# One bundle of moves at the first routing: an earlier trace of one load, a later register load, a count in two products

## The chip, the cores and the metric

One core of one Trainium2 chip. The metric is device time in microseconds (us) of one launch, lower is better. Before the change three runs took 764.91, 766.84 and 766.99 us.

## What is computed

Three layers in a row, all in float32: attention with random features, a mixture of experts with one expert per token, and a wide gated layer.

```
q_p, k_p = phi(q * scale), phi(k * scale)      # 128 exponential features per row of 64, row maximum taken off
kv = einsum('bhsm,bhsd->bhmd', k_p, v); z = sum(k_p, axis=2)
x = (q_p . kv) / (q_p . z + 1e-06)             # 4 batches x 8 heads x 576 rows x 64  ->  2304 x 512
expert = argmax(x @ w_gate); probs = softmax(x @ w_gate)
y[e] = probs[e] * (relu(x @ w1[e]) @ w2[e])    # 8 experts, 512 -> 1024 -> 512
out = (g @ w_out), g = h * sigmoid(1.702 h), h = y @ w_in      # 512 -> 2048 -> 512
```

## The kernel before, in words

The work of attention is cut into eight groups: group i holds four heads of batch i // 2. For each group `load_qk` (L247) brings k or q as a tile `m`, `halves_T` (L296) makes from it the tile `xT` with the 64 columns on the partitions, and `ph_P` multiplies it with omega. The first five tiles are turned by TensorE; the other eleven are split into two float16 halves (ScalarE the high one, L307, GpSimd the low one, L308: tile `hl`) and turned by a DMA that SyncE issues (`DMA_TRANSPOSE`, L309). `xT` has three buffers, so the turned k of group 4 takes the buffer of q of group 2 and can't start before TensorE's last read of that.

`kgen` (L390) makes the features of k in five steps (0, 1, 4, 2, 3) and `kv_ps`; `qgen` (L414) makes the features of q (steps P, tile `pr`, `qp`), turns them (X, tile `tq`), multiplies by kv (N, tile `num`) and turns the result (R, tiles `tx` and `small`), in the order of `Q_ORDER`. `route` (L523) finds a batch's most used expert: it counts the tokens of each expert with a product of ones with the one-hot matrix `oh` (`ct_ps`, L561), takes the largest (`es`), and loads it into a register of SyncE (`values_load`, L604), which the weight loads (`stage`, L674, tile `st`) use as an address. ScalarE and VectorE or GpSimd split each weight tile in two halves (`wh` L698, `wl` L700), and `moe_gen` multiplies (`m_ps`, L136).

`attention_gen` merges qgen(i), kgen(i + 1) and, after each second group, the route of the batch just finished; from the first route on, the routed expert's products are woven in by a ratio of costs. The text gives the order of tracing only: a scheduler that plays the program on its own clock sets each engine's order from it, so an edit at one place can reorder all engines behind it. In qgen(2) the k of group 4 is asked for at n == KPRE, the seventh step:

```
            if n == KPRE and i + 2 < NQ:
                load_qk(k, k_in, i + 2, asked[-1] if i == QB + 1 else None)
                halves_T(k_in, i + 2, nc.vector if i + 2 < DVE_LO else nc.gpsimd)
```

The PSUM tag "n" has one buffer, which `lg_ps`, `ct_ps` and, from group 2 on, every `num` share; "u" has one, for `tq` and `tx`; the `pr` tiles share three ("a").

Names below: P3 is the last projection of q of group 2; N0 to N4 are the `num` products of that group.

Of the kernel before, what the change touches and what calls it, by code (L numbers as in the profile page):

```python
# [22 lines left out]
def kernel(  # L23
# [13 lines left out]
    nc = tc.nc  # L37
# [6 lines left out]
    T = 4  # L44
    TAIL = S - T * P
# [16 lines left out]
    XQ = nc.sync  # L62
    DVE_LO = 1
    KPRE = 6
# [78 lines left out]
    ones = const.tile([P, P], F32, name="ones")  # L143
# [38 lines left out]
    NJ = 9  # L182
    QB = H // QH
    NQ = B * QB
    asked = []
    clock = [0]
    late = []

# [77 lines left out]
    def square_sum(m, c, sq, folds):  # L266
        nc.gpsimd.tensor_tensor(out=m[:, c], in0=m[:, c], in1=m[:, c], op=ALU.mult)
        w = D
        for _ in range(folds):
            w //= 2  # L270
            o = sq[:, c].unsqueeze(2) if w == 1 else m[:, c, 0:w]
            nc.gpsimd.tensor_tensor(out=o, in0=m[:, c, 0:w], in1=m[:, c, w:2 * w], op=ALU.add)
        if w > 1:
            nc.vector.tensor_reduce(out=sq[:, c], in_=m[:, c, 0:w], axis=AX.X, op=ALU.add)
        nc.scalar.activation(out=sq[:, c], in_=sq[:, c], func=ACTF.Copy, scale=sq_scale)
# [20 lines left out]
    def halves_T(src, i, eng):  # L296
        sides[0] += 1
        if sides[0] <= FPX:
            return turned(src, i)
        if sides[0] - 1 in LO_DVE:  # L300
            eng = nc.vector
        m = src[i]
        hl = att.tile([P, NB, 2, D], F16, tag="hl", name="hl", bufs=2)
        xT = att.tile([P, NB, P], F16, tag="xT", name="xT", bufs=3)
        sq = att.tile([P, NB], F32, tag="sq", name="sq", bufs=3)
        for c in (slice(0, 8), slice(8, NB)) if i < FINE else (slice(0, NB),):
            nc.scalar.activation(out=hl[:, c, 0], in_=m[:, c], func=ACTF.Copy)  # L307
            eng.tensor_tensor(out=hl[:, c, 1], in0=m[:, c], in1=hl[:, c, 0], op=ALU.subtract)  # L308
            XQ.dma_start_transpose(out=xT[:, c], in_=hl[:, c].rearrange("p n a d -> p (n a d)"))  # L309
            square_sum(m, c, sq, FOLD_LATE)  # L310
        src[i] = (xT, sq, False)

# [15 lines left out]
    turn = {"N": 0, "X": 0, "A": 0}  # L328
# [85 lines left out]
    def qgen(i):  # L414
        b, qd = divmod(i, H // QH)
        qi = i
        if i + 1 < NQ:
            load_qk(q, q_in, i + 1)
            halves_T(q_in, i + 1, nc.vector if i + 1 < DVE_LO else nc.gpsimd)
# [60 lines left out]
        for n, op in enumerate(Q_ORDER.split()):  # L480
            g = int(op[1])
            if op == "R0" and qd == 0:
                while x_done[0] < b - 1:
                    yield None
                xh_t[b] = (moe if b % 2 else xep).tile([P, KD, S], F32R, tag="xh", name="xh", bufs=1)
                xl_t[b] = (moe if b % 2 else xep).tile([P, KD, S], F32R, tag="xl", name="xl", bufs=1)
            if op[0] == "P":
                c = ph_P(i, src, qp, "qp", 3, g)
            else:
                c = {"X": X, "N": N, "R": XT}[op[0]](g)  # L490
            if n == 0 and i + 1 < NQ:
                load_v(i + 1)
            if n == KPRE and i + 2 < NQ:
                load_qk(k, k_in, i + 2, asked[-1] if i == QB + 1 else None)
                halves_T(k_in, i + 2, nc.vector if i + 2 < DVE_LO else nc.gpsimd)
            yield c
# [23 lines left out]
    def route_steps(b):  # L520
# [3 lines left out]
        for hf, tg in ((0, "n"), (1, "u")):  # L524
            c = slice(hf * HS, (hf + 1) * HS)
# [9 lines left out]
        for t in range(T + 1):  # L535
            n = P if t < T else TAIL
# [12 lines left out]
        nc.vector.tensor_reduce(out=rm, in_=lg, axis=AX.X, op=ALU.max)  # L549
        oh = att.tile([P, T + 1, E], F32, tag="oh", name="oh", bufs=2)  # L550
        nc.vector.tensor_tensor(out=oh, in0=lg, in1=rm.to_broadcast([P, T + 1, E]), op=ALU.is_equal)
        nc.vector.memset(oh[TAIL:, T, :], 0.0)
        ex = att.tile([P, T + 1, E], F32, tag="ex", name="ex", bufs=2)
        nc.vector.tensor_tensor(
            out=ex, in0=lg, in1=rm.to_broadcast([P, T + 1, E]), op=ALU.subtract
# [2 lines left out]
        yield 0.5  # L558
        yield 0
        ct_ps = pp.tile([P, T + 1, E], F32, tag="n", name="ct_ps", bufs=1)  # L560
        nc.tensor.matmul(  # L561
            out=ct_ps.rearrange("p t e -> p (t e)"), lhsT=ones, rhs=oh.rearrange("p t e -> p (t e)")
        )
        ct = att.tile([P, E], F32, tag="ct", name="ct", bufs=2)
        nc.vector.tensor_reduce(out=ct, in_=ct_ps.rearrange("p t e -> p e t"), axis=AX.X, op=ALU.add)
        cm = att.tile([P, 8], F32, tag="cm", name="cm", bufs=2)
# [9 lines left out]
        if b == B - 1:  # L576
            dg = att.tile([P, T * P + TAIL], F32, tag="dg", name="dg", bufs=1)
            for t in range(T + 1):
                n = P if t < T else TAIL
                nc.scalar.activation(  # L580
                    out=dg[:n, t * P:t * P + n], in_=ident[:n, :n], func=ACTF.Copy, scale=gate[:n, t, :]
# [5 lines left out]
        for t in range(T + 1):  # L587
# [9 lines left out]
            out=rr[:, :, 0:1], in0=eq, scalar=-float(2 * E), in1=ixf, op0=ALU.mult, op1=ALU.add  # L597
# [3 lines left out]
        nc.vector.tensor_tensor(out=total, in0=total, in1=hit, op=ALU.subtract)  # L601
        nc.vector.tensor_copy(rr[:, :, 1:2], gate)
        yield 0.5
        reg_t[b] = nc.values_load(  # L604
            es[0:1, 0:1], engines=[mybir.EngineType.SP], min_val=0, max_val=E - 1,
            skip_runtime_bounds_check_because="an index of the largest of E counts",
        )
        pump()
        nc.sync.dma_start(
            out=r_dram[b * S:b * S + T * P].rearrange("(p t) c -> p t c", t=T), in_=rr[:, 0:T]  # L610
# [70 lines left out]
    def pump(n=0):  # L681
        ahead = 2 * NW - 1 if prep["split"] < 2 else NST
        while prep["staged"] < min(max(prep["split"] + ahead, 2 * NW - 1), 2 * NW * B) and prep["staged"] // (2 * NW) in reg_t:
            stage(*divmod(prep["staged"], 2 * NW))
            prep["staged"] += 1
        while n and prep["split"] < min(prep["free"], prep["staged"]):
            split_w(*divmod(prep["split"], 2 * NW))
            prep["split"] += 1
            n -= 1
# [310 lines left out]
    if True:  # L1000
# [26 lines left out]
        while a_live:  # L1027
            if force == "a" or (force is None and done_a - lead <= A_RATIO * done_m):
                c = next(A, "end")
# [5 lines left out]
            else:  # L1035
                c = next(Mg)
# [363 lines left out]
        p = hp.tile([P, SETW], F32R, tag="y2", name="p2", bufs=1)  # L1400
# [29 lines left out]
    with tc.If(more > 0), tc.tile_pool(name="gp", bufs=1) as gp:  # L1430
        with tc.For_i(0, NT // P, 1) as w:
# [7 lines left out]
            xT = gp.tile([P, KD, P], F32, name="xT")  # L1439
# [13 lines left out]
            with tc.For_i(0, E, 1) as e:  # L1453
# [6 lines left out]
                with tc.If(cnt > 0):  # L1460
# [3 lines left out]
                    for f in range(NF1):  # L1464
                        wa = gp.tile([P, KD, P], F32, name="wa", bufs=2)
                        nc.sync.dma_start(
                            out=wa,
                            in_=w1[bass.ds(e, 1), :, f * P:(f + 1) * P].rearrange(
                                "o (k p) f -> p (o k) f", p=P
                            ),  # L1470
                        )
                        ps = pp.tile([P, P], F32, tag="m", name="g_ps", bufs=2)
                        for kk in range(KD):
                            nc.tensor.matmul(
                                out=ps, lhsT=wa[:, kk], rhs=xT[:, kk], start=(kk == 0), stop=(kk == KD - 1)
# [4 lines left out]
                    for dt in range(KD):  # L1480
                        wb = gp.tile([P, NF1, P], F32, name="wb", bufs=2)
                        nc.sync.dma_start(
                            out=wb,
                            in_=w2[bass.ds(e, 1), :, dt * P:(dt + 1) * P].rearrange(
                                "o (k p) d -> p (o k) d", p=P
                            ),
                        )
                        ps = pp.tile([P, P], F32, tag="m", name="g_ps", bufs=2)
                        for f in range(NF1):
                            nc.tensor.matmul(  # L1490
                                out=ps, lhsT=wb[:, f], rhs=ha[:, f], start=(f == 0), stop=(f == NF1 - 1)
# [6 lines left out]
                    for f in range(NF2):  # L1498
                        wh, wl = general_w(gp, f, 0)
                        oh, ol = general_w(gp, f, 1)  # L1500
# [44 lines left out]
```

## Time and profile before

| what | value |
|---|---|
| runs | 764.91, 766.84, 766.99 us, median 766.84 |
| the profiled execution | 766.79 us, its span 764.9 us |
| TensorE (PE) busy | 737.1 us, 96% |
| VectorE (DVE), ScalarE (ACT), GpSimd (POOL) busy | 527.5, 337.5, 131.8 us |
| weight tiles of the routed expert | 31 loads of 512 KB and 2 of 256 KB |

The page gives the busy time of each engine, the waits tell which instruction stood idle for whom, the timeline shows single instructions with start and length, and the windows add busy time and the granted TensorE clock for a stretch. Times are counted from the start of the span. A matmul's length in the timeline covers its whole way through a pipeline; the distance between starts is what one costs in a row. A `num` or `ct_ps` product shows as two records there (x4 in an order below is x8 in the trace).

### The profile page before, as it was taken

To read this page: it belongs to the slowest core of one execution; us is meant where nothing else is said; L and a number is where in the kernel's file an instruction comes from. 1 tells how busy PE (TensorE), PEld (TensorE's weight loads), DVE (VectorE), ACT (ScalarE), POOL (GpSimd) and SP (SyncE) were. 2 spreads that over 40 slices of the span, in tenths; PEclk is the share of its full clock that TensorE was granted. 3 is DMA by queue.
4 is the path that set the end of the run, shared out by engine and by line. 5 is a ranking of instruction groups with operands and counts; after the bars stand their busy time and mean duration, and the time that the engine had idled before them with its cause. 6 is when DMAs were issued, how large, how long until landed. Compare 5 with 4: busy or idle time off the path is not lost.

```text
span 764.9 us, 14360 instructions
## 1 busy us (share of the span) xinstructions
PE 737.1 (96%) x5559; PEld 715.1 (93%) x5559; DVE 527.5 (69%) x1188; ACT 337.5 (44%) x638; POOL 131.8 (17%) x78
## 2 busy tenths in 40 slices
PE   7998799998999999999999999999999999999997
PEld 6877789998999999998999999999999999999996
DVE  5866848583958577655879559981368777777774
ACT  5554554334623423332427565454576443444331
POOL 3563467604900522000000000000000000000000
PEclk9999799999999999999999999999999999999999
DMA  5447495539723544558155548972978544443311
GB/s 156 116 134 187 160 234 110 136 83 250 189 71 98 169 164 141 175 172 274 59 165 197 178 167 299 320 259 101 330 276 297 171 138 138 138 126 121 114 30 31
DMA packets 136715, 127.57 MB, mean 167 GB/s; under 512 B 58176, under 2 KB 120896, under 8 KB 135744
## 3 DMA queue, kind: packets, MB, share of 16 engines
q1 hardware_dynamic: 123936, 98.85, 44.6%
q10 hardware_dynamic: 12704, 27.73, 10.5%
q8 instruction: 45, 0.74, 0.4%
q14 instruction: 30, 0.25, 0.1%
HBM read 79.68 MB, written 40.40 MB: 157 GB/s over the span
## 4 chain that ended last, share of the span: by engine, by line
PE 80%; DMA 7%; DVE 5%; POOL 3%; ACT 2%; issue 2%; SPq 1%; ACTq 0%; POOLq 0%; DVEq 0%
PE m_ps L136 17%; PE qa L1249 13%; PE qa L1146 13%; PE qm L1249 7%; PE w_ps L136 5%; DMA st<-in_moe_w_dram 4%; PE pb L1249 3%; PE qm L1146 3%; PE qu L1146 3%; PE num L444 2%; POOL wl L700 2%; PE kv_ps L402 2%; PE qn L1146 2%; PE qt L1146 2%; DMA m<-in_k_dram 1%
## 5 line engine op out<-in xcount | busy, mean ns | idle before, releaser
L1146 PE MATMUL qa<-y,wi 128*128 128x384 f32 x576 | 109.2, 337 | 0.4 <-DVE g L901 0.4
L1146 PEld LDWEIGHTS qa<-y,wi 128*128 128x128 f32 x576 | 101.4, 188 | 0.8 <-DVE g L901 0.8
L136 PE MATMUL m_ps<-xh,wh 128*128 128x288 f32 x256 | 77.8, 304 | 0.7 <-DVE h1l L735 0.7
L136 PE MATMUL m_ps<-xh,wl 128*128 128x288 f32 x256 | 76.0, 298 | 0.0
L136 PE MATMUL m_ps<-xl,wh 128*128 128x288 f32 x256 | 75.8, 296 | 0.0
L700 POOL TENSOR_TENSOR wl<-st,wh 128x1024 fp32r<-128x1024 f32 x23 | 55.1, 2403 | 108.2 <-ACT wh L698 108.2
L359 DVE TENSOR_REDUCE small<-pr 128x4 f32<-128x512 f32 (+1 forms) x80 | 51.0, 638 | 16.1 <-PE pr L351 12.3
L698 ACT ACTIVATE wh<-st 128x1024 fp32r<-128x1024 f32 (+1 forms) x33 | 34.0, 1033 | 44.0 <-DMA st<-in_moe_w_dram 32.7
L735 DVE SCALAR_TENSOR_TENSOR h1l<-m_ps,h1h 128x288 fp32r<-128x288 f32 x64 | 28.9, 454 | 34.0 <-ACT h1h L732 34.0
L732 ACT ACTIVATE h1h<-m_ps 128x288 fp32r<-128x288 f32 x64 | 25.8, 405 | 55.3 <-PE m_ps L136 53.9
L136 PEld LDWEIGHTS m_ps<-xh,wh 128*128 128x128 f32 x256 | 48.1, 188 | 1.7 <-DVE h1l L735 1.4
L136 PE MATMUL m_ps<-h1h,wh 128*128 128x288 f32 x160 | 49.2, 307 | 0.0
L136 PEld LDWEIGHTS m_ps<-xl,wh 128*128 128x128 f32 x256 | 48.1, 188 | 0.1
L136 PEld LDWEIGHTS m_ps<-xh,wl 128*128 128x128 f32 x256 | 48.0, 188 | 0.2
L136 PE MATMUL m_ps<-h1h,wl 128*128 128x288 f32 x160 | 47.7, 298 | 0.3 <-POOL wl L700 0.3
L136 PE MATMUL m_ps<-h1l,wh 128*128 128x288 f32 x160 | 47.6, 297 | 0.0
L1249 PE MATMUL qa<-p,p 128*128 128x256 f32 x360 | 46.1, 282 | 1.1 <-DVE p L855 0.8
L1249 PE MATMUL qa<-p,gs 128*128 128x256 f32 x360 | 45.9, 282 | 0.0
L1249 PEld LDWEIGHTS qa<-p,p 128*128 128x128 f32 x360 | 44.1, 189 | 1.6 <-DVE p L855 1.0
L1249 PEld LDWEIGHTS qa<-p,gs 128*128 128x128 f32 x360 | 44.2, 189 | 0.0
L432 ACT ACTIVATE qpT<-tq 128x512 f32<-128x512 f32 (+1 forms) x40 | 22.1, 552 | 43.3 <-PE tq L430 38.6
L444 PE MATMUL num<-kv,qpT 128*128 128x65 f32 (+1 forms) x320 | 39.4, 267 | 0.7 <-ACT qpT L432 0.6
(213 smaller groups left out, 1835.1 us busy)
## 6 DMA issues: line engine op xcount, KB each, us to landing
g_dram<-g ACTq DMA_DIRECT2D x48, 384.0 KB, 3.9
st<-in_moe_w_dram SPq DMA_DIRECT2D x31, 512.0 KB, 5.0
pg<-g_dram SPq DMA_DIRECT2D x10, 1024.0 KB, 5.5
raw<-in_moe_w_in_dram SPq DMA_DIRECT2D x16, 512.0 KB, 3.8
gt<-g_dram SPq DMA_DIRECT2D x8, 1024.0 KB, 5.4
p<-wo_dram SPq DMA_DIRECT2D x6, 1024.0 KB, 7.3
yt<-y_dram SPq DMA_DIRECT2D x12, 384.0 KB, 5.4
vm<-in_v_dram SPq DMA_DIRECT2D x32, 128.0 KB, 3.2
```

The source lines that it names most:

```text
L136: ins = nc.tensor.matmul(out=ps, lhsT=a, rhs=b, start=start and n == 0, stop=stop and n == 2)
L359: nc.vector.tensor_reduce(out=pm, in_=ps[:, :w], axis=AX.X, op=ALU.max, negate=on_act)
L402: nc.tensor.matmul(out=kv_ps[:, h, :], lhsT=kp[j // 2][:, j % 2, h2, :], rhs=vm[:, h, t, :], start=(t == 0), stop=False,)
L432: nc.scalar.activation(out=qt[i][:, :w], in_=tq[:, :w], func=ACTF.Exp)
L444: nc.tensor.matmul(out=ps[:n, c, h2, :], lhsT=lhsT, rhs=kv[:, h, :])
L698: nc.scalar.activation(out=hi[:, :, s], in_=st[:, :, s], func=ACTF.Copy)
L700: eng.tensor_tensor(out=lo[:, :, s], in0=st[:, :, s], in1=f32(hi)[:, :, s], op=ALU.subtract)
L732: nc.scalar.activation(out=hh[:, f], in_=ps, func=ACTF.Relu)
L735: nc.vector.scalar_tensor_tensor(out=hl[:, f], in0=ps, scalar=0.0, in1=f32(hh[:, f]), op0=ALU.max, op1=ALU.subtract)
L1146: ins = nc.tensor.matmul(out=ps, lhsT=w[:, a, ks], rhs=y[:, b, kk], start=start and kk + m == 0, stop=kk == 1 and m == 2, skip_group_check ...
L1249: ins = nc.tensor.matmul(out=ps, lhsT=x[:, f], rhs=w[i][:, f], start=start and f + m == 0, stop=f == NP - 1 and m == 2, skip_group_check=True,
```

## The change

The k of group 4 is loaded and turned in the trace right after the first step of qgen(2) instead of the seventh (all other groups keep KPRE). The first batch's register load may not stand ahead of that turn on SyncE. For the first batch the clearing of the unused half of `oh` is gone; the count is two products, one over the four full tiles and one over the 64 rows of the last.

```
-    asked = []
+    asked, turned_last = [], [None]
...
-            XQ.dma_start_transpose(out=xT[:, c], in_=hl[:, c].rearrange("p n a d -> p (n a d)"))
+            turned_last[0] = XQ.dma_start_transpose(out=xT[:, c], in_=hl[:, c].rearrange("p n a d -> p (n a d)"))
...
-            if n == KPRE and i + 2 < NQ:
+            if n == (0 if i == QB else KPRE) and i + 2 < NQ:
...
-        nc.vector.memset(oh[TAIL:, T, :], 0.0)
+        if b:
+            nc.vector.memset(oh[TAIL:, T, :], 0.0)
...
+        full = T if b == 0 else T + 1
         nc.tensor.matmul(
-            out=ct_ps.rearrange("p t e -> p (t e)"), lhsT=ones, rhs=oh.rearrange("p t e -> p (t e)")
+            out=ct_ps[:, 0:full].rearrange("p t e -> p (t e)"), lhsT=ones,
+            rhs=oh[:, 0:full].rearrange("p t e -> p (t e)"),
         )
+        if b == 0:
+            nc.tensor.matmul(out=ct_ps[:, T], lhsT=ones[:TAIL, :], rhs=oh[:TAIL, T])
...
+        seen = len(nc.cur_bb.bb.instructions)
         reg_t[b] = nc.values_load(
             es[0:1, 0:1], engines=[mybir.EngineType.SP], min_val=0, max_val=E - 1,
...
+        if b == 0:
+            for x in nc.cur_bb.bb.instructions[seen:]:
+                tc.add_manual_dep(
+                    x, turned_last[0].ins.name,
+                    mybir.DependencyInfo(mybir.DependencyClass.NoSync, mybir.DependencyReason.DATA),
+                    reason="behind the turn",
+                )
```

SyncE, at the first routing. Before, the register load stood first, then eight weight loads, and the turn of k of group 4 (`xT_1159`) behind them; these are the last of those rows:

```order
L674 DMA st_1033<-in_moe_w2_dram 128x2x512
L609 DMA r_dram_65<-rr_1011 128x8
L674 ISA
L674 DMA st_1254<-in_moe_w2_dram 128x2x512
L612 DMA r_dram_65<-rr_1011 64x2
L309 DMA_TRANSPOSE xT_1159<-hl_1158 128x18x128
L504 DMA x_dram_63<-xn_875 64x256
L309 DMA_TRANSPOSE xT_1458<-hl_1457 128x18x128
```

Now the same turn is called `xT_902`:

```order
L258 DMA m_1453<-in_q_dram 64x2x64
L622 DMA r_dram_65<-rr_1025 128x8
L625 DMA r_dram_65<-rr_1025 64x2
L309 DMA_TRANSPOSE xT_902<-hl_901 128x18x128
L610 TENSOR_LOAD es_1000
L687 ISA
L687 DMA st_1034<-in_moe_w1_dram 128x4x128
```

The two stores of the routing result and the turn went ahead of the register load and of all weights.

TensorE, at the count (the difference, numbers of tiles left out):

```order
 L537 MATMUL lg_ps<-ident,lT 64x16
 L430 MATMUL tq<-ident,qp 128x128 x4
-L561 MATMUL ct_ps<-oh,ones 128x40
+L563 MATMUL ct_ps<-oh,ones 128x32
+L568 MATMUL ct_ps<-oh,ones 128x8
+L444 MATMUL num<-kv,qpT 128x65 x4
 L350 LDWEIGHTS xT
 L350 MATMUL pr<-wh_117,xT 128x128
```

The count became two products, and N0 came forward to stand right behind them; before, it stood behind 16 projections. Further on, the first product of the routed expert stood behind X2 and eight more projections, at row 248; now it stands at row 287, behind N4, N2 and N3, that is behind nearly all of group 2. The orders agree again over the last 1,467 of some 3,120 rows.

ScalarE, in the second batch's routing. Before (`wh2_2241` waits for a weight tile, `qpT_2331` is the last exponential of its group):

```order
L698 ACTIVATE wh1_2164<-st_2093 128x1024
L432 ACTIVATE qpT_2265<-tq_2260 128x512
L386 ACTIVATE kp_2295<-kp_2295 128x512
L386 ACTIVATE kp_2371<-kp_2371 128x512
L275 ACTIVATE sq_2496<-sq_2496 128x18
L698 ACTIVATE wh2_2241<-st_2162 128x1024
L432 ACTIVATE qpT_2331<-tq_2326 128x512
```

and now:

```order
L634 DMA row_2098<-gate_dram_64 128x640
L432 ACTIVATE qpT_2265<-tq_2260 128x512
L386 ACTIVATE kp_2295<-kp_2295 128x512
L386 ACTIVATE kp_2371<-kp_2371 128x512
L432 ACTIVATE qpT_2331<-tq_2326 128x512
L275 ACTIVATE sq_2496<-sq_2496 128x18
L711 ACTIVATE wh2_2241<-st_2162 128x1024
```

The exponential went ahead of the copy that waits for a weight tile.

## Rows read from the trace of the kernel before

**Rows 1.** Waits of TensorE, 60 to 340 us: total, times, longest.

```profile
PE ct_ps L561 <- DVE oh L552: 4.1, 1, 4.1
PE tx L464 <- ACT qpT L432: 2.2, 1, 2.2
PE pr L350 <- DMA xT<-hl: 1.9, 1, 1.9
```

**Rows 2.** Windows: length, then busy time of PE, PEld, DVE, ACT, POOL, then PEclk.

```profile
75.00:80.00 5.00, 1.20 (x12) 0.82 (x11) 4.35 (x20) 2.92 (x7) 4.84 (x4) 0.79 0.00 2
...
77.50:78.00 0.50, 0.00 (x0) 0.00 (x0) 0.50 (x3) 0.50 (x4) 0.50 (x1) 0.90 0.00 0
...
88.00:88.50 0.50, 0.50 (x9) 0.48 (x8) 0.07 (x1) 0.40 (x1) 0.00 (x0) 0.86 0.76 134
```

**Rows 3.** Timeline of VectorE (start, length, instruction), 77 to 86 us.

```profile
77.92 1.43 DVE L551 TENSOR_TENSOR oh<-lg,rm 128x40 f32<-128x40 f32 x1
...
80.10 0.07 DVE L552 MEMSET oh<- 64x8 f32 x1
...
82.36 0.18 DVE L565 TENSOR_REDUCE ct<-ct_ps 128x8 f32<-128x40 f32 x1
...
83.50 0.68 DVE L359 TENSOR_REDUCE small<-pr 128x4 f32<-128x512 f32 x1
84.10 0.14 DVE L571 CAST es<-ci 128x1 int32<-128x1 uint32 x1
...
85.47 0.17 DVE L596 SCALAR_TENSOR_TENSOR rr<-eq,ixf 128x5 f32<-128x5 f32 x1
```

**Rows 4.** Timeline of TensorE, 80 to 107 us.

```profile
80.31 0.62 PE L561 MATMUL ct_ps<-oh,ones 128*128 128x40 f32 x2 [4.12 <-DVE oh L552]
...
83.98 1.91 PE L444 MATMUL num<-kv,qpT 128*128 128x65 f32 x8
...
87.29 0.31 PE L351 MATMUL pr<-wl,xT 128*128 128x128 f16 x1
...
88.62 0.38 PE L136 MATMUL m_ps<-xh,wh 128*128 128x288 f32 x1
...
95.05 0.40 PE L136 MATMUL m_ps<-xh,wh 128*128 128x288 f32 x1
...
98.18 0.29 PE L136 MATMUL m_ps<-xh,wl 128*128 128x288 f32 x1
...
106.64 0.23 PE L350 MATMUL pr<-wh,xT 128*128 128x128 f16 x1 [1.86 <-DMA xT<-hl]
```

**Rows 5.** Timeline of SyncE's queue and of GpSimd, 70 to 100 us.

```profile
84.97 5.03 SPq L674 DMA_DIRECT2D st<-in_moe_w_dram  x8
90.10 0.88 SPq L609 DMA_DIRECT2D r_dram<-rr  x1
...
92.92 6.89 SPq L309 DMA_TRANSPOSE xT<-hl  x1
...
70.94 2.37 POOL L308 TENSOR_TENSOR hl<-m,hl 128x1152 f16<-128x1152 f32 x1 [12.70 <-DMA vm<-in_v_dram]
```

**Rows 6.** Line L309, 30 to 60 us: ns min/median/max of issuing, us to landing.

```profile
L309 SPq DMA_TRANSPOSE xT<-hl x2: 1841/2000/2160, 35.5 to 57.6; - x2
...
DMA to landing us min/median/max: 4.0/4.0/4.0
```

**Rows 7.** The same line, 90 to 107 us.

```profile
L309 SPq DMA_TRANSPOSE xT<-hl x2: 6073/6480/6886, 92.9 to 100.5; - x2
...
DMA to landing us min/median/max: 9.0/11.3/13.7
```

**Rows 8.** Timeline of ScalarE, 84 to 86 and 174 to 181 us.

```profile
84.68 1.14 ACT L376 ACTIVATE kp<-pr,mx 128x128 f32<-128x128 f32 x4 [0.65 <-DVE mx L368]
...
174.68 0.22 ACT L275 ACTIVATE sq<-sq 128x18 f32<-128x18 f32 x1
179.69 1.06 ACT L698 ACTIVATE wh<-st 128x1024 fp32r<-128x1024 f32 x1 [4.79 <-DMA st<-in_moe_w_dram]
180.65 0.58 ACT L432 ACTIVATE qpT<-tq 128x512 f32<-128x512 f32 x1
```

## The prediction

> **What bounds the kernel now.** The page comes first: TensorE is busy 737.1 of 764.9 us, so the time is its work, plus its pauses, plus what it does at half clock. The waits of TensorE say which pauses lie in the part that the change reorders [rows 1]: 4.1 us for the one-hot matrix at the first count, 2.2 us for an exponential of ScalarE near 180 us, and 1.9 us for a tile that the DMA turns. The windows tell what the first of these costs besides [rows 2]: 75 to 80 us has 1.20 us of TensorE, the granted clock goes from full to half (2.4 to 1.2 GHz) at about 77.9, while TensorE stands idle, and comes back only at about 88.1. The timelines then show who is late at each place.
>
> First place: the count starts at 80.31 [rows 4], 0.14 after the clearing on VectorE ended (80.10 + 0.07), though the comparison that makes the matrix was over at 77.92 + 1.43 = 79.35 [rows 3]. Second place: the register load lets the weights go at 84.97; the turn of k of group 4, whose halves were ready at 70.94 + 2.37 = 73.31, is issued behind them at 92.92 [rows 5], needs 6.89 us of SyncE and lands after 13.7 us [rows 7], at 106.6. There TensorE waits from 104.78 to 106.64 [rows 4]. Third place: ScalarE is to copy a weight tile that lands at 179.69, and the exponential behind it, for which it was ready at about 175, comes at 180.65 [rows 8]; the one PSUM buffer that it would free is what TensorE lacks for 2.2 us.
>
> **The change part by part.** The sum is made against the profiled execution, 766.79 us, which stands at the median of the runs (766.84).
>
> *Count.* Without the clearing the product can start at 79.35 + 0.14 = 79.49, 0.8 us earlier. The second product costs at most what the whole count shows, 0.62 us [rows 4], and at least a record's distance, 0.1; I take 0.4. Behind them now stands N0, which needs the buffer that the count was in, so TensorE pauses until VectorE has read it. VectorE reads it at about 80.65, right behind the index searches, instead of 82.36 [rows 3], because the conversion and the `qp` step went behind it. N0 then runs from 80.9 to 82.8 (1.91 us at half clock [rows 4]). The 0.8 us is thus used by work that before came at 83.98: no term of its own. The index is ready about 1.0 us earlier (83.2 for 84.24), the routing result at 84.2 for 85.64.
>
> *P3, on which the turn waits.* The turn needs the buffer of q of group 2, so TensorE's last projection P3 must be over; before, that was at 87.29 + 0.31 = 87.60 [rows 4]. P3 takes the `pr` buffer that ScalarE's exponentials of k's second step free (1.14 us from 84.68 [rows 8]); their maximum moved behind the routing result, from 83.50 [rows 3] to about 84.6, so they end at 86.9. TensorE's own list up to P3 is, from 82.8 at half clock, about 5.7 us (one N at 1.91, two transposes, 20 projections), so 88.5, and P3 ends at 89.3. If the clock came back earlier, P3 ends at 87.5, on the exponentials. TensorE has no gap from 80.9 on here, while before it had one of 0.5 at 82; so I take 88.4 between the two bounds.
>
> *SyncE's queue.* The two stores of the routing result go ahead (0.88 us for the first [rows 5]); they are over before 86 and cost nothing while the turn waits for P3. The turn takes 2.0 us of SyncE and lands after 4.0 [rows 6] when no weights are under way, 6.89 at worst [rows 7]. Nothing large is under way then, so 2.0: 90.4. Register load and first weights follow as before, 84.97 - 84.24 = 0.73 us behind the last thing that they wait for: 91.2 for 84.97, **6.2 us later**. From the first weight load to the first routed product it was 88.62 - 84.97 = 3.65 us; now that product comes at 94.85.
>
> *What covers these 6.2 us.* The list between P3 and the first routed product holds X2, N4, N2, X3, N3 and 24 projections: about 6 us of TensorE at full clock (an N at half of 1.91, the rest likewise), and for VectorE three reductions at 0.68 [rows 3] and about as much again in subtractions and normalising, some 6.6 us. So N3 ends near 94.5: TensorE is nearly filled, and what is put off is the routed products that filled the same time before. If that cover were gone, all 6.2 us would be lost.
>
> *Where both have done the same.* Before, at 104.78 TensorE had done all this and 72 routed products, which at 24 in 3.26 us (95.05 to 98.18 + 0.13 [rows 4]) make 9.8 us. Now: 94.85 + 9.8 + 0.4 for transposes that follow + 0.5 for small waits = 105.5. The turned k has landed at 88.4 + 4.0 = 92.4 and isn't waited for, where before it held TensorE until 106.64. **Gain 1.1 us** (bounds: 2.4 with P3 at 87.5 and no small waits; a loss of 4 with 6.89 us for the turn).
>
> On this the Trainium skill (DMA: Bandwidth & Descriptors, Issuing engines are not separate DMA queues) says that transfers share the same 16 DMA engines and interleave: the turn ahead of the weights would then slow the first weights rather than be slowed. The trace agrees that they hurt one another [rows 6, 7]. By that rule the first weights, which overlap the turn from 91.2 to 92.4, would come up to 1.2 us later, and the gain would be about nil.
>
> *ScalarE's order.* The exponential now stands ahead of the copy that waits for its weights, so at about 175 it runs at once and TensorE's wait near 180 goes: **gain 2.2 us** [rows 1]. What is late next there is the copy itself; the transposes that need ScalarE after it come some 6 us later in the list.
>
> *The rest.* Loads of v went ahead of loads of k and q of group 5, which start about 3 us later; nobody waited for them in [rows 1]. Reordered instructions up to about 310 us can make new pauses; the order before had only the 2.2 and two of 0.3 there. Bounds 0 and 2.5; I take 0.4.
>
> Sum: 766.79 - 1.1 - 2.2 + 0.4 = **763.9 us**.
>
> **The rivals.**
>
> *The pause near 180 stays or moves.* For it: the weights' landing, not the order alone, sets ScalarE's time, and another instruction could stand behind the next copy. Against: the order shows exactly this pair exchanged. Then 763.9 + 2.2 = 766.1.
>
> *The weights come too late and attention doesn't fill the gap: slower.* The mechanism is SyncE's queue: register load and weights sit behind a turn that waits for P3. It decides from the first routed product at 96 us, where the gain at the meeting point is gone; each us beyond costs one. With 6.89 us for the turn that product comes at 99.7, a loss of 3.8 against a gain of 1.1: 768.8 with the pause near 180 gone, 771.0 without; 769.5 in between. Against: nothing is under way when the turn goes out. For: cover of VectorE that is full to the brim, and an N that waits for one PSUM buffer each time. The Trainium skill (DMA: Bandwidth & Descriptors, Rules for kernel authors) speaks for this rival: issue a DMA early and wait for it late; the change does so for the turn and the contrary for 4 MB of weights. No row shows the weights issued late.
>
> *The turn wasn't the limit.* TensorE's wait at 106.64 could pass to a `pr` buffer at the same place, and the change would give only a reorder: about 766.5.
>
> **How the numbers follow.** A measurement tells about 0.3%, 2.3 us, from no change; against the median that is faster below 764.5 and slower above 769.1. The forecast has a chance of 0.55, the first rival 0.22, the slower one 0.15, the last 0.08. Of the forecast's cases about nine in ten lie below 764.5, of the others hardly any: faster 0.51. Of the slower rival's cases some three quarters pass 769.1: 0.12. The rest, 0.37, is no change. The range goes from 762.0 (both gains at their better bounds: 766.79 - 2.4 - 2.2) to 768.0, which takes in the first and the last rival and leaves out the slower one.
>
> **What would show it.** In the profile after: the count near 79.5; the turn issued at 87.5 to 89.5, 2 us long, landing in 4 to 5; first weights at 90 to 92; first routed product at 94 to 96, TensorE nearly busy before it; no wait for `xT` after it; no wait of `tx` near 180. It is wrong if a window between 88 and 96 shows TensorE idle by over 2 us, if the turn takes over 4 us of SyncE, if a full clock is lost again behind that gap, or if the waits of TensorE up to 310 us add up to over 3 us in new places.

## The result and the profile after

The changed kernel took 772.01 us (median of ten runs, 769.41 to 774.17), the kernel before 766.91 beside it (762.80 to 769.53): ratio 1.0072, 95% interval 1.0048 to 1.0096. It is **slower by 0.7%**; the forecast was 763.9 us with a range to 768.0. A repeat of the same pair (after_again below) gave 1.0063 (1.0035 to 1.0091). The profiled execution took 771.85 us, its span 770.0, which is 5.1 more than before.

The page's line on busy time (us, share of the span, instructions) answers to 737.1 us of TensorE before:

```profile
PE 740.0 (96%) x5561; PEld 717.2 (93%) x5561; DVE 526.8 (68%) x1187; ACT 338.5 (44%) x638; POOL 131.9 (17%) x78
```

TensorE's waits from 60 to 340 us (total, times, longest) answer to [rows 1]:

```profile
PE pr L350 <- DVE qp L380: 3.5, 1, 3.5
PE ct_ps L563 <- DVE ex L555: 3.3, 1, 3.3
PE m_ps L136 <- DVE h1l L748: 1.9, 1, 1.9
PE tq L430 <- DVE xl L473: 1.2, 1, 1.2
PE tx L464 <- DVE xl L473: 1.1, 1, 1.1
```

The two waits that the forecast removed are gone: 2.2 us for `qpT`, 1.9 us for the turned tile. But 3.5 + 1.9 + 1.2 + 1.1 = 7.7 us stand in places where before had nothing of note.

**At the first routing it went as foretold.** SyncE's queue and TensorE there, answering to [rows 5] and [rows 4]:

```profile
85.26 2.06 SPq L309 DMA_TRANSPOSE xT<-hl  x1
88.58 5.37 SPq L687 DMA_DIRECT2D st<-in_moe_w_dram  x8
```

```profile
77.17 0.60 PE L563 MATMUL ct_ps<-oh,ones 128*128 128x32 f32 x2 [3.29 <-DVE ex L555]
...
92.22 0.40 PE L136 MATMUL m_ps<-xh,wh 128*128 128x288 f32 x1
...
115.34 0.40 PE L136 MATMUL m_ps<-xh,wh 128*128 128x288 f32 x1 [1.85 <-DVE h1l L748]
...
194.75 0.27 PE L350 MATMUL pr<-wh,xT 128*128 128x128 f16 x1 [3.48 <-DVE qp L380]
196.20 1.11 PE L430 MATMUL tq<-ident,qp 128*128 128x128 f32 x4 [1.18 <-DVE xl L473]
```

This execution is 2.3 us ahead of the other when it reaches the change (the first `lg_ps` product starts at 72.41 for 74.73). 1.8 of that stand by 67 us, after the other lost its full clock near 50 us (below); the rest is a wait for `xl` that is 0.5 us here and 1.0 there. With 2.3 added, turn, first weights and first routed product stand at 87.6, 90.9 and 94.5, where the text had 88.4, 91.2 and 94.85.

**At the second routing, near 195 us, it went wrong.** Windows (length, then busy time of PE, PEld, DVE, ACT, POOL, PEclk, DMA share, GB/s), the first two from the first routing:

```profile
85.00:90.00 5.00, 4.21 (x47) 3.55 (x45) 5.00 (x19) 1.21 (x3) 0.00 (x0) 1.00 0.54 123
90.00:95.00 5.00, 4.51 (x41) 3.81 (x38) 4.01 (x13) 4.04 (x11) 0.00 (x0) 1.00 0.93 278
191.00:193.00 2.00, 0.28 (x3) 0.16 (x3) 0.58 (x2) 2.00 (x4) 1.62 (x1) 0.92 0.96 171
193.00:195.00 2.00, 0.24 (x1) 0.00 (x0) 1.93 (x6) 1.64 (x4) 2.00 (x2) 0.50 0.94 329
195.00:197.00 2.00, 0.82 (x5) 0.80 (x5) 1.71 (x5) 1.25 (x2) 2.00 (x2) 0.50 0.90 281
197.00:199.00 2.00, 2.00 (x15) 1.79 (x14) 1.90 (x6) 1.63 (x4) 2.00 (x2) 0.50 1.02 185
199.00:201.00 2.00, 2.00 (x20) 1.93 (x18) 1.84 (x6) 0.41 (x1) 2.00 (x2) 0.88 0.80 273
```

The kernel before has in the whole of that stretch:

```profile
191.00:201.00 10.00, 9.73 (x95) 9.42 (x95) 9.43 (x25) 7.32 (x12) 10.00 (x5) 1.00 0.91 250
```

From 191 to 197 us TensorE works 1.34 of 6 us. Its granted clock falls to half (2.4 to 1.2 GHz) at about 192.7, in the first of these pauses, and is back at about 199.5. Who is late is read backwards, first on VectorE and then on ScalarE:

```profile
184.01 0.42 DVE L455 TENSOR_TENSOR xn<-num,rd 128x256 f32<-128x256 f32 x1
192.39 0.23 DVE L473 TENSOR_TENSOR xl<-small,xh 128x64 fp32r<-128x64 f32 x1 [7.95 <-ACT xh L469]
...
194.01 0.69 DVE L380 TENSOR_TENSOR qp<-pr,mx 128x512 f32<-128x512 f32 x1
```

```profile
181.30 1.06 ACT L711 ACTIVATE wh<-st 128x1024 fp32r<-128x1024 f32 x1 [7.40 <-DMA st<-in_moe_w_dram]
...
186.34 1.06 ACT L711 ACTIVATE wh<-st 128x1024 fp32r<-128x1024 f32 x1 [3.38 <-DMA st<-in_moe_w_dram]
...
190.14 1.16 ACT L307 ACTIVATE hl<-m 128x1152 f16<-128x1152 f32 x1 [2.74 <-DMA y_dram<-y]
191.21 1.04 ACT L711 ACTIVATE wh<-st 128x1024 fp32r<-128x1024 f32 x1
192.15 0.21 ACT L469 ACTIVATE xh<-small 128x64 fp32r<-128x64 f32 x1
```

The second pair of `xh` copies of group 4 (192.15 is its first; TensorE had made its input by 184.3) stands on ScalarE behind two copies that wait for transfers, a weight tile's and that of k of group 7, and a third that does not. (For k's the row names a store of `y`; the copy's input is `m`, k's load.) VectorE waits 7.95 us for `xh`; behind that wait stand the `qp` steps, behind those TensorE's projections. The copy at 181.30 held the first pair in the same way, which is the wait of 1.1 us at `tx`.

The kernel before has the second pair behind the same two kinds of copies, a weight tile's and that of k:

```profile
188.73 1.06 ACT L698 ACTIVATE wh<-st 128x1024 fp32r<-128x1024 f32 x1 [2.90 <-DMA st<-in_moe_w_dram]
189.71 1.16 ACT L307 ACTIVATE hl<-m 128x1152 f16<-128x1152 f32 x1
190.78 0.21 ACT L469 ACTIVATE xh<-small 128x64 fp32r<-128x64 f32 x1
```

There VectorE waits 2.00 us for that `xh`, and TensorE has no wait over 0.3 us from 185 to 210. New in the order is only the third copy in front of the pair (186.34; before, that tile's copy stands ahead of the first pair, at 184.17). What is new besides is time: the input of `xh` is there at 184.3 for 187.7, while k's copy ends at 191.3 for 190.9.

A small wait of the same kind stands in the first routing, ahead of 115.34 above: the gate's row, which goes out to memory and back, holds ScalarE for 3.21 us, and the eviction `h1h` of the routed layer stands behind it:

```profile
113.33 1.16 ACT L643 ACTIVATE gb<-row 128x512 f32<-128x512 f32 x2 [3.21 <-DMA row<-gate_dram]
114.40 0.40 ACT L745 ACTIVATE h1h<-m_ps 128x288 fp32r<-128x288 f32 x1
```

### The profile page after: what moved, and what is told of

The parts are those of the page before. It is cut to its first block, busy times and chain, and to the rows that moved or that the text cites. A ratio compares the mean times of both kernels' runs of the same rounds, so it can differ in the third digit from the quotient of the medians.

```text
span 770.0 us, 14365 instructions
## 1 busy us (share of the span) xinstructions
PE 740.0 (96%) x5561; PEld 717.2 (93%) x5561; DVE 526.8 (68%) x1187; ACT 338.5 (44%) x638; POOL 131.9 (17%) x78
## 4 chain that ended last, share of the span: by engine, by line
PE 83%; DMA 7%; DVE 6%; ACT 1%; POOL 1%; issue 1%; SPq 1%; DVEq 0%; ACTq 0%; POOLq 0%
PE m_ps L136 18%; PE qa L1262 13%; PE qa L1159 13%; PE qm L1262 7%; PE w_ps L136 5%; PE pb L1262 3%; PE qm L1159 3%; PE qu L1159 3%; DMA st<-in_moe_w_dram 3%; PE num L444 3%; PE kv_ps L402 2%; PE pr L344 2%; PE qn L1159 2%; PE qt L1159 2%; DMA m<-in_k_dram 1%; PE tq L430 1%
## 5 line engine op out<-in xcount | busy, mean ns | idle before, releaser
L444 PEld LDWEIGHTS num<-kv,qpT 128*128 128x128 f32 (+1 forms) x320 | 36.8, 184 | 4.4 <-issue 2.4
```

The source lines that it names most:

```text
L444: nc.tensor.matmul(out=ps[:n, c, h2, :], lhsT=lhsT, rhs=kv[:, h, :])
```

## What TensorE lost, by stretch

To compare kernels whose orders differ, the trace of each was cut into windows of half a us: length less busy time, plus busy time times (1 - granted clock), is what TensorE lost. The last column is the page's busy time less the half-clock part. All in us, one profiled execution each; the kernels are those of the experiments below.

| kernel | to 56 | 56-160 | 160-210 | 210-400 | busy, at full clock |
|---|---|---|---|---|---|
| before | 9.2 | 12.5 | 2.4 | 1.9 | 731.7 |
| changed | 7.6 | 11.1 | 7.5 | 3.4 | 733.6 |
| changed, again | 7.7 | 9.4 | 8.0 | 2.0 | 733.3 |
| changed, no wait for the turn (no_dep) | 8.9 | 12.4 | 3.8 | 1.6 | 731.8 |
| changed, count as before (move_dep) | 7.3 | 15.5 | 3.7 | 1.6 | 731.7 |
| the same with rules (move_dep_rules) | 10.8 | 18.5 | 4.1 | 2.3 | 730.0 |
| changed, rules, k later (after_k_later_copies2) | 9.0 | 10.9 | 2.1 | 1.6 | 733.7 |
| that, no wait for the turn (move_count_rules) | 11.2 | 12.9 | 0.6 | 1.6 | 730.7 |
| before, exchange, rules (before_exchange_copies2) | 7.3 | 10.0 | 0.4 | 1.7 | 731.8 |

Executions with the first routing's order of before lie between 8.6 and 12.5 in the second column, so the forecast's 1.1 us there can't be seen in one profile. Six kernels with the changed order show 733.2 to 733.7 us of work at full clock, all others 730.0 to 732.0. Those 2 us have no place that could be named: ends of matmuls are modelled, and a product that follows one of another kind takes some 0.1 us more between starts (in the new order the tile written changes 623 times from one product to the next, 606 before). But move_dep, with 616 of these changes, shows 731.7 us. Whether the 2 us are work or reckoning stays open.

## The experiments

In the expectations, theory A is ScalarE's queue at the second routing, C the third weight tile there (its load now stands behind that of k of group 7 on SyncE), D the late register load and weights, B the late weights or the pace of the second routing's weight transfers; other rivals are described where they stand. `follow(x, y)` puts x behind y in its engine's order, without a semaphore.

### A: ScalarE's queue

**after_copies_first**: the changed kernel, with the fifth weight copy of the second batch and the halves of k and q of group 7 behind that second pair of `xh` copies ("rule 1").

```
+            for x in first if i == NQ - 1 else ():            # halves_T, high half
+                follow(hi, x)
...
+                if qi == 2 * QB and pr == 1:                  # XT, the xh copies of group 4
+                    first.append(c)
...
+                for x in first if (b, c) == (1, 4) else ():   # split_w
+                    follow(copy, x)
```

> The changed kernel, whole, with one more rule at the second routing: the copies that end the output of group 4 (xh from small and tx) may not stand behind the weight copy wh4 and the halves of k and q of group 7 on ScalarE. Theory A (the loss lies in that queue: copies that wait for transfers hold VectorE and so TensorE): the pauses of 3.5 and 1.2 us near 191 to 196 go and the clock stays full there, so 4.7 us idle and some 1.8 us at half clock come back: 765.5 to 768, no wait of pr for qp over 1 us at 185 to 200. Theory B (the late weights of the first routing, or the pace of the second routing's weight transfers, cost the time): the pause only moves to a wait for weights, 770.5 to 773.

766.26 us, 1.0025 (0.9993 to 1.0057). The 3.5 and the 1.2 us went; TensorE's waits from 160 to 210 us now begin with another:

```profile
PE tq L433 <- ACT qpT L435: 2.8, 1, 2.8
PE tx L467 <- DVE xl L478: 0.8, 1, 0.8
```

The exponential `qpT` stands behind the next copies that wait for transfers:

```profile
195.27 1.16 ACT L308 ACTIVATE hl<-m 128x1152 f16<-128x1152 f32 x1 [2.37 <-POOL hl L311]
196.62 1.06 ACT L716 ACTIVATE wh<-st 128x1024 fp32r<-128x1024 f32 x1 [0.18 <-DMA st<-in_moe_w_dram]
198.37 0.59 ACT L435 ACTIVATE qpT<-tq 128x512 f32<-128x512 f32 x1
```

**before_copies_first**: rule 1 on the kernel before.

> The kernel before, with the same rule added. It has no TensorE pause at 190 to 200, so by theory A there is nothing to win: 766 to 768. If the rule is worth something by itself, whatever the change did, this falls by 2 us or more too, and the gain of the other run says less. Theory B: 766 to 768 as well.

764.96 us, 1.0012 (0.9982 to 1.0042). There too the rule takes the `xh` pair out from behind the copies that wait for transfers (VectorE's wait of 2.00 us goes), but TensorE had no pause from it, and the time doesn't change.

**after_copies_first2**: rule 1, and the sixth weight copy and the halves of q of group 7 behind the first exponential of group 5 ("rules").

```
+            for x in first + (second if sides[0] == 2 * NQ else []) if i == NQ - 1 else ():   # halves_T
+                follow(hi, x)
...
+            if qi == 2 * QB + 1 and i == 0:                   # X, the exponential
+                second.append(c)
...
+                for x in first if (b, c) == (1, 4) else second if (b, c) == (1, 5) else ():
+                    follow(copy, x)
```

> The changed kernel with the rule of the earlier run and a second one: the weight copy wh5 and the halves of q of group 7 stand behind the first exponential (qpT) of group 5 on ScalarE, since with the first rule alone TensorE paused 2.8 us there (tq for qpT) and lost the full clock again. Theory A (the loss is ScalarE's queue at the second routing): that pause goes with its 1.7 us at half clock; 2 to 4 us below the run with one rule, 762 to 764.5, no pause of TensorE over 1.5 us from 185 to 210. Theory B (the pace of the weight transfers): the pause passes to m_ps waiting for wh or wl, no gain, 765 to 768.

769.21 us, 1.0061 (1.0037 to 1.0084), where theory A had expected 762 to 764.5. The profiled execution lost 4.7 us in 160 to 210, where the changed kernel beside it (**after_again**, no edit) lost 8.0:

> The changed kernel unaltered, beside the others of this call, so that differences of a few us are taken on one chip. Both theories: 1.005 to 1.010 of the kernel before.

769.72 us, 1.0063. So the queue on ScalarE is what makes the pauses, for each rule moves them; but with the pauses smaller the time is 0.4% better with one rule and hardly better with both. The intervals of the two overlap; why their medians stand 0.4% apart is open. Theory A explains the trace near 195 us and not the whole loss.

### C: the third weight tile

**after_k_later**: the changed kernel, the load of k of group 7 behind the third weight load of the second batch.

```
-                load_qk(k, k_in, i + 2, asked[-1] if i == QB + 1 else None)
+                load_qk(k, k_in, i + 2, asked[-1] if i == QB + 1 else third[0] if i == NQ - 3 else None)
...
+                if (b, c) == (1, 2):                          # stage, the third weight load
+                    third.append(ins)
```

> Theory A (ScalarE's queue alone) fell short: with both of its rules the changed kernel stayed at 1.006. Theory C: on SyncE, at the second routing, the reorder put the load of k of group 7 ahead of the third weight tile; its copy on ScalarE came 17.8 to 18.6 us after the first weight load of that routing in all kernels of the changed order, 13.0 to 14.5 in all of the old one, and every copy behind it is late with it. Here the changed kernel gets one rule: that load of k stands behind the third weight tile on SyncE. Theory C: third copy 14 to 16 us after the first load, pauses of TensorE at 185 to 205 under 2.5 us instead of 4.7, 1.000 to 1.004 of before. If the load of k was not it (theory D: the first routing's part of the change itself costs 4 to 5 us, by weights that come later): 1.005 to 1.007.

768.55 us, 1.0054 (1.0035 to 1.0073), though the third copy now came 15.3 us after the first load (176.72 - 161.38) where the changed kernels had 17.8 to 18.6. **after_k_later_copies2** adds the rules:

> The same, with the two rules on ScalarE's copies too, so that only the first routing differs in kind from the kernel before with exchange and both rules. Theory C: 0.993 to 0.999 of before, near that kernel. Theory D: 1.000 to 1.006, 4 us or more above that kernel.

766.04 us, 1.0029 (1.0007 to 1.0051): the stretch from 160 to 210 is as good as before (2.1 for 2.4 us lost), and 0.3% stays. Against the two rules without it (1.0061, 4.7 us lost there) it is 0.3% faster, with intervals that overlap.

**before_exchange_copies2_k_first**: the contrary, that load ahead of the third weight load in a kernel without the change (the next experiments' best one).

```
+            if src is k and i == NQ - 1:
+                follow(third[0], k_ins[-1])
```

> The fastest so far with the load of k of group 7 forced ahead of the third weight tile (the turn of q of group 6 goes ahead of it too), that is the changed kernel's fault put into a kernel whose first routing is the old one. Theory C: third copy 17 to 19 us after the first load of that routing, 3 to 6 us slower than without: 1.000 to 1.004 of before. Theory D: no more than 1 us slower.

760.45 us, 0.9969 (0.9948 to 0.9991). The third copy is as late as in the changed kernel, 17.7 us after the first load, with no loss at all (0.9972 without the rule on that load, below):

```profile
160.74 1.02 SPq L688 DMA_DIRECT2D st<-in_moe_w_dram  x2
...
172.65 0.58 SPq L256 DMA_DIRECT2D m<-in_k_dram  x1
...
178.44 1.06 ACT L714 ACTIVATE wh<-st 128x1024 fp32r<-128x1024 f32 x1 [6.27 <-DMA st<-in_moe_w_dram]
```

A late third copy is thus not enough to cost time; theory C falls as the cause of the loss. In the changed kernel the place of that load may still be worth the 0.3% above.

### The exchange by itself

**before_exchange**: the kernel before with one pair on ScalarE exchanged, the last exponential of group 4 ahead of the third weight copy: the forecast's 2.2 us alone.

```
+            if qi == 2 * QB and i == 3:                       # X, the last exponential of group 4
+                follow(weight[0], c)
...
+                if (b, c) == (1, 2):                          # split_w, the third copy
+                    weight.append(copy)
```

> The kernel before with nothing but the exchange that the prediction counted as 2.2 us: the last exponential of group 4 ahead of the copy wh2 on ScalarE. If the 2.2 us are a gain by themselves: 762 to 763. Theory A: TensorE comes 2 us earlier to the same queue, whose copies wait for transfers, and gives the lead back as a pause of pr or tq between 185 and 200, with a chance of a lost clock (1.7 us): 764 to 766.5.

763.75 us, 0.998 (0.9959 to 1.0001): some 1.5 us, not quite told from nothing. Of the 2.2 us for `qpT` at `tx`, 1.5 came back at the same place, now for `xl`, and two of 0.6:

```profile
PE tx L467 <- DVE xl L476: 1.5, 1, 1.5
PE tq L431 <- ACT qpT L433: 0.6, 1, 0.6
PE tq L431 <- DVE qp L381: 0.6, 1, 0.6
```

**before_exchange_copies2** adds the rules; **before_exchange_copies2_again** is the same kernel once more.

> The exchange and both rules on the kernel before. Theory A: nothing holds TensorE there, so the 2.2 us stay won: 761 to 763. Theory B: 764 to 766, with waits for weights. Whichever is right, beside the run of the changed kernel with both rules it tells what the first routing's part of the change (turn first, weights later, count in two) is worth alone: the prediction says that one is 1.1 us faster.

> The fastest so far, unaltered, beside the others of this call: 0.993 to 0.998 of before by all theories.

760.70 us, 0.995 (0.9917 to 0.9983), and 762.56 us, 0.9972 (0.9949 to 0.9996): **faster than both kernels**, by 0.3 to 0.5% than the one before. Second routing, 160 to 210 us:

```profile
160.00:210.00 50.00, 49.60 (x458) 47.64 (x457) 36.72 (x113) 25.62 (x46) 30.44 (x14) 1.00 0.78 200
```

The changed kernel has in the same 50 us:

```profile
160.00:210.00 50.00, 44.25 (x389) 41.84 (x388) 32.20 (x103) 22.44 (x39) 28.11 (x13) 0.93 0.82 186
```

### The parts of the change

**count_only**: before, with the clearing gone and the count in two products. **move_dep**: the changed kernel with clearing and one product put back, that is the earlier tracing of k and the register load behind the turn.

```
-            if n == (0 if i == QB else KPRE) and i + 2 < NQ:    # count_only
+            if n == KPRE and i + 2 < NQ:
...
-        if b == 0:
-            for x in nc.cur_bb.bb.instructions[seen:]:
-                tc.add_manual_dep(
...
-        full = T if b == 0 else T + 1                           # move_dep
+        full = T + 1
```

> The kernel before with the count in two products and no clearing for the first batch, nothing else: the weights go out as before, ahead of the turn. Theory A: what matters is what order the scheduler then makes of the second routing; here the exponential also goes ahead of the weight copy, the halves of k of group 7 stand ahead of the last small copy but wh4 behind it, so a pause of 0 to 3 us near 190: 765 to 769. Theory B: no late weights, so no loss: 765 to 767, and the wait of 1.9 us for xT near 105 is there.

> The changed kernel with the one-product count and the clearing put back: the turn still goes ahead of the register load and the weights. Theory A: the order at the second routing is nearly that of the changed kernel (halves of k of group 7, wh4, then the small copy), so a pause of 2 to 5 us at 188 to 200: 769 to 773. Theory B: late weights again: 770 to 773. If it is at 767 or under, the count is what makes the loss.

count_only 766.74 us, 1.0033 (1.0008 to 1.0057); move_dep 769.36 us, 1.0066 (1.0038 to 1.0094), nearly the whole loss. As any edit reorders the second routing as well, the parts were run again with the rules, which hold ScalarE's order there. **count_alone_rules**: count_only, rules, k later. **move_alone_rules**: before with the earlier tracing alone, rules and the exchange. **move_count_rules**: the changed kernel without the wait for the turn, rules, k later. **move_dep_rules**: move_dep, rules, k later.

```
-        if b == 0:                                              # move_count_rules: gone
-            for x in nc.cur_bb.bb.instructions[seen:]:
-                tc.add_manual_dep(
-                    x, turned_last[0].ins.name,
```

> Of the change only the count in two products without the clearing, weights ahead of the turn. Theory D: 0.994 to 0.999. If the count (TensorE's order behind it, with N0 right behind the count) is what costs: 1.000 to 1.004.

> All four kernels of this call carry the rules at the second routing (exponential ahead of the weight copy, output copies and first exponential of group 5 ahead of copies that wait for transfers), so that they differ in the first routing's part. Here of the change only the earlier trace of the turn: the register load stays ahead of it, the count is one product. Theory D (the weights that come later, behind the turn, are what costs): as the kernel before with the rules, 0.994 to 0.998 of before. Theory A (only the second routing ever cost): the same.

> The changed kernel without the rule that holds the register load behind the turn: trace move and count, weights early. Theory D: 0.994 to 0.999. Theory A: 0.994 to 1.003, as the whole change with the rules (1.0029).

> The changed kernel with the one-product count put back: turn first, weights late. Theory D: 1.001 to 1.005, with waits of TensorE for wh or h1l between 85 and 125 us that add up to 2 us or more, absent in the kernels of this call whose weights go first. Theory A: 0.994 to 0.998.

| kernel | us | ratio (95%) | first weight load, us |
|---|---|---|---|
| count_alone_rules | 762.19 | 0.9981 (0.9961 to 1.0001) | 80.4 |
| move_alone_rules | 765.58 | 1.0018 (0.9983 to 1.0053) | 81.7 |
| move_count_rules | 763.17 | 0.9993 (0.9973 to 1.0014) | 84.5 |
| move_dep_rules | 770.50 | 1.0091 (1.0053 to 1.0129) | 91.5 |

Against the kernel before, the count, the earlier tracing and the two together show no loss; with the register load held behind the turn the loss is there. But these kernels have the rules, and the kernel before with exchange and rules is itself faster, at 0.9950, 0.9972 and (k first) 0.9969: against that the three lie 0.1 to 0.7% higher, with intervals that overlap or touch. move_alone_rules, expected at 0.994 to 0.998, came out at 1.0018, and move_count_rules just above its 0.994 to 0.999. So a part of the loss may sit in the earlier tracing. move_dep_rules came out above its 1.001 to 1.005, too. It shows the waits that were expected of it in TensorE's list from 84 to 132 us, 2.1 + 1.5 us for `h1l` and `wh`:

```profile
PE m_ps L136 <- DVE h1l L755: 2.1, 1, 2.1
PE m_ps L136 <- ACT wh L716: 1.5, 1, 1.5
PE tq L434 <- DVE qp L384: 0.6, 1, 0.6
PE num L450 <- DVE xn L461: 0.6, 1, 0.6
```

**no_dep** and **count_rules_two**: the changed kernel without the wait for the turn and nothing else; and count_only with the rules, the load of k where the scheduler puts it.

> The changed kernel without its last part alone, the rule that holds the register load behind the turn; no rules of ours at the second routing. The weights go out at once again. Theory D: 0.999 to 1.003. If the other two parts carry the loss after all: 1.005 to 1.008.

> Candidate for the best version: the kernel before with the count in two products and the two rules on ScalarE's copies, without the rule on the load of k. 0.994 to 0.999; it beats the exchange with both rules (0.995 and 0.997) only if the count is worth something.

no_dep 765.66 us, 1.0019 (0.9996 to 1.0042); count_rules_two 764.53 us, 0.9995 (0.9977 to 1.0012). no_dep starts its weights at 82.8 us, the changed kernel at 88.58. Its waits from 84 to 132 us, and its second routing:

```profile
PE tq L430 <- ACT qpT L432: 1.9, 1, 1.9
PE pr L350 <- ACT kp L376: 0.5, 1, 0.5
PE m_ps L136 <- ACT wh L704: 0.2, 1, 0.2
```

```profile
160.00:210.00 50.00, 47.88 (x430) 46.39 (x428) 34.11 (x120) 22.85 (x41) 30.25 (x14) 0.97 0.75 189
```

**The rule that holds the register load behind the turn costs time.** Three pairs differ in it, and so in when the weights start:

| kernels | weights late | weights early |
|---|---|---|
| the whole change | 1.0072, again 1.0063 | 1.0019 (no_dep) |
| with rules and k later | 1.0029 | 0.9993 (move_count_rules) |
| no count, with rules | 1.0091 | 1.0018 (move_alone_rules) |

That is 0.4 to 0.7%, 3 to 5 us, the same way in all three, though the two intervals of a pair overlap a little. The first pair differs in nothing else in the text, the second neither; the third also in the exchange and the place of k's load. As only the third pair was measured side by side, ratios to the kernel before are compared.

That it costs because the weights come late isn't shown. The rule also reorders every engine: between the changed kernel and no_dep TensorE's order differs from 85 to 261 us, ScalarE's in some 80 of 638 instructions from 83 to 256 us, at the second routing too. One sign that speaks for the late weights lies in the first routing: TensorE's wait for `h1l` is 0.9 to 2.1 us in seven of the eight profiles with late weights, and 0.4 or less in eleven of the twelve with early ones (the others 0.2 and 0.9); yet in the changed kernel the wait ahead of 115.34 is one for the gate's row, and the same kernel again has 0.2. And there is a sign against: with the count and early weights (five kernels) TensorE waits 1.7 to 2.6 us for `qpT` in the same stretch, which no kernel with late weights does. The rest of the loss takes other forms: without the count, pauses at the first routing (15.5 and 18.5 us lost from 56 to 160); with it, pauses at the second and the 2 us of busy time. Whether the rule leads to these by the scheduler's order or by later transfers, no run here tells.

## Why the prediction was wrong

- *Count*: right. At 77.17, or 79.5 with the 2.3 us; the second product came 0.54 us behind the first (estimate 0.4).
- *P3, turn and queue*: right within 0.8 us. P3 ended at 85.2, with the 2.3 us at 87.5, the text's better bound, as the full clock was back at 83.4. The turn took 2.06 us of SyncE (taken: 2.0) and landed after 4.0.
- *First weights and cover*: right. From the first weight load to the first routed product 3.64 us (3.65); TensorE busy 4.21 and 4.51 of 5 us from 85 to 95, at full clock. The gap there that the slower rival needed didn't come.
- *Gain of 1.1 us at the meeting point*: the wait for the turned tile is gone, and the 1.85 us for `h1l` at 115.34 stand close behind it. The stretch lost 11.1 for 12.5 us, within the scatter.
- *Gain of 2.2 us near 180*: the wait went as said (`qpT` at 173.19, ahead of the copy at 181.30). But in before_exchange it is alone worth some 1.5 us (0 to 3 by the interval), because `xl` is late next; the text asked what is late next and answered with the copy, not with what stands behind it.
- *The rest, 0.4 us (bounds 0 and 2.5)*: **this term failed**. From 160 to 210 us the changed kernel lost 7.5 us. Before lost 2.4 there, 2.2 of which the forecast had taken off, so some 7.3 us came for 0.4, a lost full clock among them. What failed is the reason given for the small term, that the order before had no other pauses there: TensorE and VectorE now came some 3 us earlier to ScalarE's copies that wait for transfers, and the second `xh` pair of group 4 stands behind them, behind two in the order before and three in the new one. The text had read one pair of that order. The text named the sign to look for, new waits over 3 us in sum; 7.7 came. From 210 to 400 us the profile lost 1.5 us more than before, with a lost full clock at 356.5; the second profile of the changed kernel doesn't have that (2.0 us). The 2 us more of work at full clock are in no term.
- *The slower rival* named the rule that the runs find to cost time, and its 768.8 to 771.0 came nearest to the 772.0. But its mechanism didn't come: the turn took 2.06 us and not 6.89, and idle time ahead of the first routed product shows in move_dep_rules (1.5 us for `wh`) and not in the changed kernel. That it came near in time is thus partly luck. Its chance of 0.15 was too low: the text itself said that no row showed the weights issued late, and that the cover was full to the brim.

The Trainium skill (DMA: Bandwidth & Descriptors, Rules for kernel authors) says to issue a DMA early and wait late. The runs point the same way: the rule that held 4 MB of weights some 6 us cost 0.4 to 0.7%, though they don't separate the lateness from the order that came with it. It also says (Perfetto Trace Analysis, Tensor Engine Instruction (MATMUL, LD_WEIGHTS)) that ScalarE's queue is strictly first in, first out; the 7.95 us that VectorE above waits for ScalarE's `xh` fit that.

## What to carry to other kernels

Where an engine that evicts also makes copies of tiles from a DMA, read its whole order in the stretch that a change rearranges: each copy that waits for a transfer holds every eviction behind it, and an exchange of one pair can just move the wait to the next. The order alone doesn't give the price, though: ask when each engine will come to such a copy, for a lead won earlier can be given back there. Don't hold a large load back to give a small one a free queue on a sum that has no row for it. And when a change moves one thing and reorders a hundred more, run its parts, with the reordered stretch held still by explicit order.

## What was not expected of the hardware

A loss of the full clock costs much the same in different kernels: near 50 us before, after_k_later_copies2 and no_dep lose 1.7 us each, and move_count_rules, at half clock from 49.0 to 55.8, twice that. The same order in that stretch loses it in some executions and not in others. Before:

```profile
50.00:52.00 2.00, 2.00 (x10) 1.91 (x11) 1.90 (x8) 2.00 (x5) 1.22 (x1) 0.65 0.06 13
52.00:54.00 2.00, 2.00 (x8) 1.62 (x8) 1.60 (x6) 0.12 (x1) 1.80 (x1) 0.50 0.00 0
```

and before_exchange_copies2, which differs only later:

```profile
50.00:52.00 2.00, 2.00 (x14) 1.76 (x13) 1.97 (x9) 1.43 (x3) 0.87 (x2) 1.00 0.00 0
52.00:54.00 2.00, 2.00 (x14) 1.66 (x13) 1.37 (x6) 1.29 (x4) 1.92 (x2) 1.00 0.00 0
```

At the first count the loss comes in two sizes: four of the nine profiles with the one-product count, before among them, are at half clock for 10.2 us there and the other five for 6.8, while all eleven with the count in two have 6.8. The lost clock is much of why one execution of a kernel differs from the next, and why a gain of 1 us can't be read from one profile of each.
